# First-pass experts five to eight of the second mixture moved from hand-written units to the plan, with their weight sums split ahead

## The chip, the cores and the metric

One core of a Trainium2 chip runs the whole program in one launch. The metric is device time in microseconds (us): the median of three runs. A profiled execution of the same program gives the rows below; its own time and its span (first to last instruction) stand in the table.

## What is computed

Three layers, all in float32: a retention layer (4 batches, 8 heads, 576 positions of 64), a mixture with the best of eight experts for each token, and a mixture in which every token goes through all eight experts, weighted by a Sinkhorn-normalised gate. The third is most of the time:

```python
# x: 2304 x 512; w1: 8 x 512 x 1024; w2: 8 x 1024 x 512
out = np.zeros((N, D), dtype=np.float32)
for e in range(E):
    h = np.maximum(x @ w1[e], 0.0)
    ye = h @ w2[e]
    out += P[:, e:e + 1] * ye
```

## The kernel before

Every float32 operand is split into a high and a low part of a shorter format (ScalarE casts the high part, VectorE subtracts it from the operand for the low part: `lo_of`, L237), and a product is three matmuls, high x high, high x low and low x high.

**The second mixture** takes its 2304 tokens in three passes of 768, and in each pass the eight experts one after the other. The first product of an expert (`x @ w1`) is a 2 x 2 block product in seven instead of eight block products, from sums and differences of the blocks of `w1` ("sums") and of the tokens. The sums of one quarter of an expert's `w1` (i = 0 to 3) are 1792 columns, high and low. They are made once, in the first pass, and stored to DRAM in `w1s`; the later passes load them from there.

*First pass, hand-written units.* `unit` (L1243) is one quarter of one expert: seven block products (L1260 to L1262, 384 columns each, six matmuls to a product) and between them the second product of the quarter before (`second`, L1179; L1190 to L1192, 512 columns each, an ordinary product, nine matmuls for three token tiles at a time). There are 32 units. The order of a unit on TensorE is product 0, three token tiles of `second`, products 1 and 2, three tiles, product 3, three tiles, products 4 and 5, three tiles, product 6. Products 0, 2, 3 and 4 add up in one PSUM bank, which ScalarE copies out after 0, 2 and 3 (`keep`, L1238: `p1`, `u2`, `u3`); the next of these products waits for the copy. `mid` is called at named places ("p0", "b", ...) and runs what `mids` has for that place: the gate's steps and the tokens of the next pass.

*The ring.* Weights arrive by SP's DMA queue in five buffers of 512 KB (`raw`, `load_more`, L233) and are split into a ring of four slots (`split_step`; four steps to a slot). "plain" slots are cast as they are (L260); "sums" slots go through four sums on GpSimd (L271, L272) first (cast L279). A slot of first weights of the second mixture is stored to `w1s` at the start of its unit (L1248), high and low part, 896 KB each. `take` hands the next slot out and emits what is left of its splits; `release` gives a slot back. The first mixture uses the same ring for its own weights, four slots to an expert: two for `gemm1` (eight half-products of 12 matmuls with a ReLU after each), two for `gemm2`. A model of the two clocks (`clock`, `arrives`) decides where split steps are emitted.

*Second and third pass, planned.* From expert `s = E` on, every piece of work is a `Task` with an engine, a cost and predecessors. TensorE's order is written out (`line`); the other engines take the task with the earliest due time. A planned expert has the same first product (L1543 to L1545, weights `wa` loaded from `w1s` at L1510), and a second product that is also one of seven block products (L1690 to L1692, 256 columns each); its weights are combined on GpSimd (L1448, L1451) and split (L1636 on ScalarE, L237 on VectorE). `load_pass` brings in and splits the tokens of the next pass; between passes one and two that is done by the units (`xload`, `xsums`, and `xsplit` in the last unit through `renew`), between two and three by the plan. The buffers of the plan are laid over the ring and the work buffers of the units when these are done.

## Time and profile before

| | |
|---|---|
| median of 3 runs | 1811.48 us (1811.03 to 1811.97) |
| profiled execution, its own time | 1811.14 us |
| its span | 1809.4 us |
| TensorE matmul busy | 1785.6 us, 12398 matmuls |
| VectorE, ScalarE, GpSimd busy | 1244.2, 891.4, 409.4 us |
| DRAM read and written | 248.26 and 74.79 MB, 179 GB/s over the span |

The span has three parts: retention layer and first mixture up to 338 us, the first pass of the second mixture in units up to 842, the planned passes to the end. Matmuls are pipelined, so the busy time of TensorE says little; the starts of successive matmuls give what one costs. A line number alone belongs to the kernel before.

### The profile page before, as it was taken

The page shows a single profiled execution, that of the slowest core. Times are in us where ns is not written, and L with a number is a line of the kernel's source. Part 1 is how long each engine was busy: PE and PEld are TensorE (multiplying, and loading weights), DVE is VectorE, ACT ScalarE, POOL GpSimd, SP SyncE. Part 2 cuts the span into 40 slices and gives each one's busy share as a digit, 9 for nine tenths or more (in the row PEclk, how much of TensorE's full clock was granted, in tenths as well). Part 3 has the DMA queues.
Part 4 walks back from the last instruction along what each step waited for, and adds up shares of the span by engine and source line. Part 5 has one row for each costly group of instructions (what it writes and reads, how often), then busy time and mean ns, then how long its engine had stood idle before and what let it go on. Part 6 is the DMA issues. An engine that isn't in the chain of part 4 may idle for free.

```text
span 1809.4 us, 32670 instructions
## 1 busy us (share of the span) xinstructions
PE 1785.6 (99%) x12398; PEld 1705.3 (94%) x12398; DVE 1244.2 (69%) x2205; ACT 891.4 (49%) x1718; POOL 409.4 (23%) x396
## 2 busy tenths in 40 slices
PE   8999999999999999999999999999999999999998
PEld 7889999998999999998999999999999999999997
DVE  6764666557555655664667787787877777777777
ACT  2454455534443333343565555555656555555553
POOL 4630121221321212213221111111222112111212
PEclk9999999999999999999999999999999999999999
DMA  9854655564545556545755556555555555555540
GB/s 325 298 196 158 213 184 190 186 217 155 197 176 192 192 192 227 185 164 188 234 155 169 158 163 191 166 163 153 150 182 181 162 164 153 177 160 156 155 129 36
DMA packets 190597, 325.29 MB, mean 180 GB/s; under 512 B 20551, under 2 KB 93400, under 8 KB 190429
## 3 DMA queue, kind: packets, MB, share of 16 engines
q1 hardware_dynamic: 187132, 312.89, 53.2%
q0 software_dynamic: 3136, 9.95, 1.6%
q8 instruction: 100, 1.64, 0.4%
q14 instruction: 69, 0.56, 0.1%
q10 hardware_dynamic: 160, 0.26, 0.0%
HBM read 248.26 MB, written 74.79 MB: 179 GB/s over the span
## 4 chain that ended last, share of the span: by engine, by line
PE 86%; DVE 3%; issue 2%; ACT 1%; POOL 0%; POOLq 0%; DVEq 0%; ACTq 0%
PE b L1543 8%; PE b L1545 8%; PE b L1544 8%; PE b L1692 8%; PE b L1691 8%; PE b L1690 8%; PE b L1190 5%; PE b L1192 5%; PE b L1191 5%; PE b L1260 4%; PE b L1261 4%; PE b L1262 4%; PE b L722 4%; PE b L724 3%; PE b L723 3%
## 5 line engine op out<-in xcount | busy, mean ns | idle before, releaser
L1691 PE MATMUL b<-wb,sq 128*128 128x256 f32 x1344 | 378.5, 282 | 1.1 <-DVE wb L237 1.1
L1690 PE MATMUL b<-wb,sq 128*128 128x256 f32 x1344 | 377.1, 281 | 0.9 <-DVE a L1712 0.9
L1692 PE MATMUL b<-wb,sq 128*128 128x256 f32 x1344 | 377.1, 281 | 0.4 <-DVE sq L237 0.4
L1691 PEld LDWEIGHTS b<-wb,sq 128*128 128x128 f32 x1344 | 254.0, 189 | 1.7 <-DVE wb L237 1.7
L1692 PEld LDWEIGHTS b<-wb,sq 128*128 128x128 f32 x1344 | 254.4, 189 | 0.6 <-DVE sq L237 0.6
L1690 PEld LDWEIGHTS b<-wb,sq 128*128 128x128 f32 x1344 | 252.9, 188 | 1.8 <-issue 1.3
L237 DVE TENSOR_TENSOR ring<-raw,ring 128x512 fp32r<-128x512 f32 (+1 forms) x256 | 192.5, 761 | 69.2 <-ACT ring L260 61.0
L237 DVE TENSOR_TENSOR sq<-hq,sq 128x768 fp32r<-128x768 f32 x167 | 168.8, 1015 | 68.3 <-ACT sq L1636 68.2
L1448 POOL TENSOR_TENSOR raw<-raw,raw 128x512 f32<-128x512 f32 x60 | 84.8, 1414 | 384.2 <-DVE wb L237 313.3
L1558 ACT ACTIVATE hq<-hq 128x384 f32<-128x384 f32 x144 | 75.6, 526 | 184.4 <-DVE hq L1555 183.7
L1543 PE MATMUL b<-ch,wa 128*128 128x384 f32 x448 | 151.4, 338 | 2.2 <-DVE hq L1555 1.6
L1260 PE MATMUL b<-ch,ring 128*128 128x384 f32 x448 | 152.5, 340 | 0.2
L1543 PE MATMUL b<-c,wa 128*128 128x384 f32 x448 | 151.2, 337 | 1.1 <-ACT u L1549 1.1
L1636 ACT CAST sq<-hq 128x768 fp32r<-128x768 f32 x167 | 137.6, 829 | 29.2 <-PE b L1691 24.5
L1545 PE MATMUL b<-ch,wa 128*128 128x384 f32 x448 | 150.6, 336 | 0.0
L1545 PE MATMUL b<-c,wa 128*128 128x384 f32 x448 | 150.6, 336 | 0.0
L1261 PE MATMUL b<-cl,ring 128*128 128x384 f32 x448 | 150.6, 336 | 0.0
L1262 PE MATMUL b<-ch,ring 128*128 128x384 f32 x448 | 150.6, 336 | 0.0
L1544 PE MATMUL b<-cl,wa 128*128 128x384 f32 x448 | 150.6, 336 | 0.0
L1544 PE MATMUL b<-c,wa 128*128 128x384 f32 x448 | 150.5, 336 | 0.0
L1190 PE MATMUL b<-ring,HH 128*128 128x512 f32 x384 | 149.8, 390 | 0.0
L1192 PE MATMUL b<-ring,HL 128*128 128x512 f32 x384 | 149.5, 389 | 0.0
(258 smaller groups left out, 4179.5 us busy)
## 6 DMA issues: line engine op xcount, KB each, us to landing
wa<-w1s SPq DMA_DIRECT2D x192, 512.0 KB, 4.2
raw<-in_moe_w_dram SPq DMA_DIRECT2D x128, 512.0 KB, 3.9
w1s<-ring SPq DMA_DIRECT2D x64, 896.0 KB, 5.9
raw<-in_moe_w_dram SPq DMA_DIRECT2D x106, 256.0 KB, 3.5
wa<-w1s SPq DMA_DIRECT2D x64, 256.0 KB
sums<-in_moe_w_dram SPq DMA_DIRECT2D x22, 256.0 KB, 3.2
xs<-x SPq DMA_DIRECT2D x19, 256.0 KB, 4.8
kT<-in_kT_dram SPq DMA_DIRECT2D x18, 256.0 KB, 4.0
```

Source lines behind the costliest of these rows:

```text
L237: eng.tensor_tensor(lo, x, hi.bitcast(F32), ALU.subtract)
L1190: nc.tensor.matmul(y[t], hh[:, s], w.hi[:, f0:f0 + 512], start=first, stop=False)
L1192: nc.tensor.matmul(y[t], hl[:, s], w.hi[:, f0:f0 + 512], start=False, stop=end)
L1260: nc.tensor.matmul(ps, a, xh[:, r, :], start=first and r == 0, stop=False, skip_group_check=True)
L1261: nc.tensor.matmul(ps, a, xl[:, r, :], start=False, stop=False, skip_group_check=True)
L1262: nc.tensor.matmul(ps, b, xh[:, r, :], start=False, stop=r == 1, skip_group_check=True)
L1543: nc.tensor.matmul(ps, a, xh[:, r, :], start=first, stop=False, skip_group_check=True)
L1544: nc.tensor.matmul(ps, a, xl_[:, r, :], start=False, stop=False, skip_group_check=True)
L1545: nc.tensor.matmul(ps, b, xh[:, r, :], start=False, stop=r == 1, skip_group_check=True)
L1690: nc.tensor.matmul(ps, hh[:, r, c], wh[:, r], start=st, stop=False, skip_group_check=True)
L1691: nc.tensor.matmul(ps, hh[:, r, c], wl[:, r], start=False, stop=False, skip_group_check=True)
L1692: nc.tensor.matmul(ps, hl[:, r, c], wh[:, r], start=False, stop=kh == 1 and r == 1, skip_group_check=True)
```

## The change

- The plan begins at expert `S0 = 4` of the first pass (it was `E`, the first expert of the second pass). There are 16 units instead of 32. The tokens of the second pass are now brought in by `load_pass`, in the plan; `renew`, the token loads in `mids` and the flag `last` go.
- The sums of the first weights of experts 4 to 7 (16 quarters) have to be in `w1s` before the plan loads them. Eight of them are made in the first mixture, as extra slots of the ring (`make_ahead`; `MADE_IN` says how many in which expert): loaded, summed, split like a unit's slot and stored at once by `store_sums`, then the slot is free again. Ring slots are now handed out from a list of free ones.
- The other eight are made beside units 9 to 16 with buffers of their own (`side_tiles`: two load buffers `er`, one for sums `ez`, two for the split `ec`). In unit k of these, at "p0" to "p3", piece s is cast and subtracted (`side_cut`) and the piece before is stored (`side_store`); at "p4" the last piece is stored and the weights of two units later are loaded; at "d" GpSimd makes the next sums. The source is read in rows of 128 columns (512 bytes).

```diff
+    S0 = 4
+    MADE_IN = (0, 1, 2, 2, 1, 1, 1, 0)
...
+    made = [(e, i) for e in range(S0, E) for i in range(4)]
+
+    def make_ahead():
+        e, i = made.pop(0)
...
+        Slot("sums", [part((e, i, 0), source)], 0, store=4 * e + i)
 
     for i in range(E):
         w1_slots(i)
-        w2_slots(i)
...
+        for f in range(2):
+            if MADE_IN[i] > f:
+                make_ahead()
+            w2_slot(i, f)
+    for e in range(S0):
...
+    ring_free, held = [1, 0, 2, 3], []
...
-            if j >= min(len(slots), n_rel[0] + RING):
+            if j >= len(slots) or (s == 0 and not ring_free):
                 return
...
             if s == 0:
-                c.hi, c.lo = (ringt[j % RING][:, 2048 * n:2048 * (n + 1)] for n in range(2))
+                c.ring = ring_free.pop(0)
+                c.hi, c.lo = (ringt[c.ring][:, 2048 * n:2048 * (n + 1)] for n in range(2))
...
             n_split[0] += 1
+            if s == 3 and c.store is not None:
+                store_sums(c, c.store)
+                ring_free.append(c.ring)
...
+    def store_sums(c, n):
+        for k, x in enumerate((c.hi, c.lo)):
+            nc.sync.dma_start(out=w1s[n][:, k], in_=x[:, 0:1792].bitcast(F32))
+        arrives(5.2)
...
+    def side_load(k):
+        if 0 <= k < len(made):
+            e, i = made[k]
+            for h in range(2):
+                nc.sync.dma_start(out=aside["raw"][k % 2][:, h], in_=w21[e][:, h * half + 128 * i:h * half + 128 * (i + 1)]
+                                  .rearrange("(k p) f -> p k f", p=128))
+            arrives(1.46)
+
+    def side_sums(k):
+        if 0 <= k < len(made):
+            first_sums(aside["z"], *(aside["raw"][k % 2][:, h] for h in range(2)))
+
+    def side_cut(k, s):
+        fa, fb = (aside["raw"][k % 2][:, h] for h in range(2))
+        z = aside["z"]
+        x = (fa, fb[:, 2:4], z[:, 0:4], z[:, 4:8])[s]
+        n = 128 * x.shape[1]
+        hi, lo = (aside["cut"][s % 2][:, h, 0:n].rearrange("p (j f) -> p j f", f=128) for h in range(2))
+        nc.scalar.copy(hi, x)
+        lo_of(nc.vector, lo, x, hi)
+
+    def side_store(k, s):
+        e, i = made[k]
+        o, n = ((0, 512), (1024, 256), (512, 512), (1280, 512))[s]
+        nc.sync.dma_start(out=w1s[4 * e + i][:, :, o:o + n], in_=aside["cut"][s % 2][:, :, 0:n].bitcast(F32))
+        arrives(1.5)
+
+    def side_mids(k):
+
+        def cut_at(s):
+            if s:
+                side_store(k, s - 1)
+            side_cut(k, s)
+        m = {} if k < 0 else {f"p{s}": (lambda _, s=s: cut_at(s)) for s in range(4)}
+
+        def end(_):
+            if k >= 0:
+                side_store(k, 3)
+            side_load(k + 2)
+            if k < 0:
+                side_load(k + 1)
+        m["p4"] = end
+        m["d"] = lambda _: side_sums(k + 1)
+        return m
...
-    n_unit = E * 4
+    n_unit = S0 * 4
...
-        elif p + 1 < NP and e == E - 3 and i == 3:
-            mids = {k: (lambda b, n=n: xload(p + 1, n)) for n, k in enumerate("bc")}
-        elif p + 1 < NP and e == E - 2 and i > 1:
-            mids = {"b": lambda b, n=i - 2: xsums(n)}
+        elif g >= n_unit - len(made) - 1:
+            mids = side_mids(g - n_unit + len(made))
...
-    for s in range(E, n_exp):
+    for s in range(S0, n_exp):
```

Two places in the order of instructions, both of the third expert of the first pass. First ScalarE in the tenth unit, from its first copy on (`c` are the copies p1, u2 and u3 out of PSUM bank `b0`, `HH` a ReLU, `ring` the splits). Before:

```order
L1238 COPY c_7320<-b0_7313 128x384
L279 CAST ring3_71<-raw4_67 128x512
L1228 ACTIVATE HH_111<-c_7347 128x384
L279 CAST ring3_71<-raw0_63 128x256
L1238 COPY c_7359<-b0_7313 128x384
L279 CAST ring3_71<-sums_84 128x512
L1238 COPY c_7378<-b0_7313 128x384
```

With the change (`er`, `ez` and `ec` are the side stream's buffers):

```order
L1278 COPY c_7482<-b0_7475 128x384
L1400 CAST ec0_6344<-er1_6342 128x512
L308 CAST ring3_71<-raw2_65 128x512
L1268 ACTIVATE HH_111<-c_7511 128x384
L308 CAST ring3_71<-raw3_66 128x256
L1400 CAST ec1_6345<-er1_6342 128x256
L1278 COPY c_7526<-b0_7475 128x384
L1400 CAST ec0_6344<-ez_6343 128x512
L308 CAST ring3_71<-sums_84 128x512
L1278 COPY c_7548<-b0_7475 128x384
```

A cast of the side stream now stands behind each copy or ahead of it; the third one, which writes `ec0` again, stands between the copies u2 and u3.

Then SP's queue from the ninth unit's pair of stores on (`w1s<-ring x2` is a unit's pair; loads of `raw` stand between the pairs). Before, up to the pairs of the tenth and eleventh unit:

```order
L1248 DMA w1s_90<-ring0_78 128x1792 x2
L233 DMA raw0_63<-in_moe2_w1_dram 128x4x256
L233 DMA raw1_64<-in_moe2_w2_dram 128x2x512
L233 DMA raw2_65<-in_moe2_w2_dram 128x2x512
L233 DMA raw3_66<-in_moe2_w1_dram 128x4x256
L1248 DMA w1s_90<-ring1_79 128x1792 x2
L1248 DMA w1s_90<-ring3_71 128x1792 x2
```

With the change, up to the pair of the tenth unit:

```order
L318 DMA w1s_90<-ring1_79 128x1792 x2
L254 DMA raw3_66<-in_moe2_w1_dram 128x4x256
L254 DMA raw4_67<-in_moe2_w2_dram 128x2x512
L1406 DMA w1s_90<-ec0_6344 256x1x512
L1406 DMA w1s_90<-ec1_6345 256x1x256
L1406 DMA w1s_90<-ec0_6344 256x1x512
L254 DMA raw0_63<-in_moe2_w2_dram 128x2x512
L254 DMA raw1_64<-in_moe2_w1_dram 128x4x256
L1406 DMA w1s_90<-ec1_6345 256x1x512
L1386 DMA er0_6341<-in_moe2_w1_dram 128x4x128 x2
L318 DMA w1s_90<-ring2_80 128x1792 x2
```

Four stores and two loads of the side stream now stand between two pairs; two loads of `raw` stand ahead of the unit's first side store and two ahead of its fourth, and the next unit's pair stands behind the side loads.

## Rows read from the trace of the kernel before

**Rows 1.** The page, part 1, whole span: engines' busy time, share, instructions; TensorE's clock by slices

```profile
span 1809.4 us, 32670 instructions
...
PE 1785.6 (99%) x12398; PEld 1705.3 (94%) x12398; DVE 1244.2 (69%) x2205; ACT 891.4 (49%) x1718; POOL 409.4 (23%) x396
...
PEclk9999999999999999999999999999999999999999
```

**Rows 2.** Stretches: from:to, length, busy PE, PEld, DVE, ACT, POOL (instructions), clock, DMA, GB/s

```profile
470.08:841.66 371.58, 371.58 (x1874) 336.66 (x1874) 216.80 (x346) 149.90 (x312) 80.52 (x95) 1.00 0.51 183
882.28:1235.88 353.60, 353.60 (x2521) 353.60 (x2521) 263.91 (x401) 193.09 (x346) 60.26 (x47) 1.00 0.55 167
1235.88:1356.41 120.53, 119.05 (x842) 118.22 (x841) 99.58 (x149) 67.92 (x119) 30.26 (x24) 1.00 0.54 164
...
173.00:236.00 63.00, 63.00 (x435) 60.94 (x434) 36.11 (x59) 30.91 (x64) 9.97 (x8) 1.00 0.61 201
```

**Rows 3.** Time line of TensorE, second products of a unit and a planned expert: start, length

```profile
661.06 0.39 PE L1190 MATMUL b<-ring,HH 128*128 128x512 f32 x1
...
663.10 0.34 PE L1260 MATMUL b<-ch,ring 128*128 128x384 f32 x1
...
1200.78 0.28 PE L1690 MATMUL b<-wb,sq 128*128 128x256 f32 x1
...
1201.49 0.34 PE L1543 MATMUL b<-ch,wa 128*128 128x384 f32 x1
```

**Rows 4.** Waits of TensorE, 841 to 884: waiter, releaser, sum, count, longest

```profile
PE b L1543 <- DVE hq L1555: 1.6, 2, 1.0
PE b L1543 <- ACT u L1549: 0.6, 1, 0.6
```

**Rows 5.** Time line of TensorE and ScalarE, one unit

```profile
655.88 0.34 PE L1260 MATMUL b<-ch,ring 128*128 128x384 f32 x1
...
661.30 0.60 ACT L260 CAST ring<-raw 128x512 fp32r<-128x512 f32 x1
661.81 0.47 ACT L1238 COPY c<-b 128x384 f32<-128x384 f32 x1
...
666.18 0.34 PE L1260 MATMUL b<-ch,ring 128*128 128x384 f32 x1
```

**Rows 6.** Time line of SP, two issues

```profile
669.24 0.37 SPq L233 DMA_DIRECT2D raw<-in_moe_w_dram  x1
...
680.89 1.05 SPq L1248 DMA_DIRECT2D w1s<-ring  x2
```

**Rows 7.** DMA issues of 470 to 840: count, KB each, median us from issue to landing

```profile
w1s<-ring SPq DMA_DIRECT2D x46, 896.0 KB, 5.9
raw<-in_moe_w_dram SPq DMA_DIRECT2D x42, 512.0 KB, 3.8
```

**Rows 8.** Stretches in which only stores, 1 KB loads, 2 KB loads move (columns of rows 2)

```profile
681.70:686.00 4.30, 4.30 (x24) 3.85 (x23) 2.15 (x3) 1.27 (x3) 2.84 (x4) 1.00 1.02 427
686.50:688.00 1.50, 1.50 (x10) 1.50 (x10) 1.15 (x3) 0.31 (x2) 0.00 (x0) 1.00 0.90 300
720.20:721.20 1.00, 1.00 (x6) 0.85 (x5) 0.80 (x2) 0.44 (x1) 0.00 (x0) 1.00 1.00 383
```

**Rows 9.** Time line of GpSimd and VectorE, a sum and two subtractions

```profile
661.74 1.06 POOL L271 TENSOR_TENSOR sums<-raw,sums 128x256 f32<-128x256 f32 x1
...
662.12 1.22 DVE L237 TENSOR_TENSOR ring<-raw,ring 128x512 fp32r<-128x512 f32 x1
...
668.52 0.69 DVE L237 TENSOR_TENSOR ring<-raw,ring 128x512 fp32r<-128x512 f32 x1
```

110 lines of the change are left out of this document (61 added, 49 removed).

## The prediction

> **What bounds the kernel now.** I read the first part of the page first, to see that TensorE is busy for 99% of an 1809.4 us span at the full clock, with the others far below [rows 1]. So a change gains only by fewer or shorter matmuls and loses only where TensorE is made to wait. Then the table by stretches: each row has its length, and the matmuls in brackets behind PE's busy time. Six experts of the hand-written part take 371.58 us, 61.93 each, with 1874 matmuls (312 each and two at the edge); six planned experts take 353.60 us, 58.93 each, with 2521 (420 each) [rows 2]. The planned expert has more matmuls and is shorter. The time line of TensorE says why: nine matmuls of 512 columns start within 2.04 us, 0.227 each, and six of 256 columns within 0.71 us, 0.118 each [rows 3]. A second product takes 144 of the first kind (32.7 us) in a unit expert, 252 of the second (29.8 us) in a planned one. The first product is the same in both.
>
> **The sum, part by part.** It is made against the profiled execution (1811.14 us, span 1809.4, so 1.74 around it); the median of the runs, 1811.48, lies 0.34 above it.
>
> *Four experts move to the plan.* 4 x (61.93 - 58.93) = **-12.0 us** [rows 2]. The hand-over itself, last unit beside first planned expert, occurs once in both kernels. By the Trainium skill ("TensorE: Matmul & The Clock Gate", Back-to-back issue gap) matmuls follow each other after N/2.4 + 2.5 ns, which is 216 and 109 ns, 3.6 us an expert and -14.2 for four (an estimate by that page). The rows have 227 and 118 with the weight loads, so they decide.
>
> *The change of token pass moves into the plan.* Between passes one and two the units split the new tokens in the last unit, and the stretch shows no loss. The planned change of pass costs 120.53 - 2 x 58.93 = 2.67 us [rows 2]; now there are two of these: **+2.7 us**.
>
> *Hand-over.* Now 0.62 and 1.6 us of waits stand there, on ScalarE and VectorE [rows 4]. The last unit loses seven token splits and gets four small cuts; the first planned loads of `wa` no longer wait for the ring slot that the last unit reads, but stand behind the side stream's last store on SP. A little earlier work on VectorE's queue: **-0.6**, between -2.2 (all of these waits) and +2.2 (as much again).
>
> *Eight sums in the first mixture's ring.* Each adds four casts, four subtractions, four GpSimd sums, a load of 512 KB and two stores of 896 KB. Experts three and four (63 us) get four of them. ScalarE is busy for 31 and VectorE for 36 of the 63 us, and stay under the span with four times 3 us more. The queue is the risk: its share is 0.61 [rows 2], 38.4 us, and each sum adds 4.3 us of stores and some 2 of load (rates below): 38.4 + 4 x 6.3 = 63.6 of 63 us. A ring slot just stored is split again four half-products later (12 matmuls of 0.145 each, 63 us over 435, so 7 us), against 5.9 us for a store to land [rows 7]; where a cast waits there, what stands behind it is ScalarE's last ReLUs before the second product, and TensorE goes on from other banks. With no load late the price is 0. With 7.6 us a sum instead of 6.3 the queue overflows by 5.8 us. Taken: **+1.0**, near the lower end, because slots are split a few us ahead of use.
>
> *The side stream.* In units 9 to 16, ScalarE casts a piece into one of two cut buffers, VectorE subtracts, SP stores, and the third cast needs the first store landed. That is the new wait, and behind it on ScalarE stand a split and then the copy `u3`, for which product 4 waits. In the trace the copy follows a split's cast by 0.51 us and takes 0.47, and product 4 starts at 666.18, 10.3 after the unit's start at 655.88 [rows 5]. So the third cast must start by 10.3 - 0.51 - 0.51 - 0.47 - 0.1 = 8.7 us into the unit. When does the store land? All loads and stores pass one queue in order. Its rates [rows 8]: 427 GB/s for the 896 KB stores (7 KB pieces), 383 for 2 KB pieces, 300 for 1 KB; so 4.3 us for a pair of stores, 1.4 for 512 KB in 2 KB pieces, 1.7 in 1 KB. The stores issued at 680.89 move from 681.7: 0.8 us to the first byte [rows 6, 8]. Side loads come in 512-byte pieces, which this trace lacks: at least 1.2 us (the 427 GB/s row), at most 3.5 (twice the packets of a 1 KB load); I take 2.0, near the 1 KB row and below its rate. A landing counts 0.3 us after the last byte (0.2 to 1.3, the latter what 3.8 us for a 512 KB load to land [rows 7] leave over 0.8 and 1.7).
>
> Tenth unit: on SP a load of `raw` stands ahead of the ninth unit's fourth side store; such a load goes at 669.24, 13.4 into its unit [rows 6], and holds SP till then. It moves until 15.9; fourth piece 17.3; side loads 19.3; the next unit's pair 23.6; the first piece 25.0, landed 25.3, which is 9.8 into the tenth unit: **1.1 us late**. Eleventh: the fourth piece is released 3.7 us before the unit ends (cut behind `u3`), moves to -1.5, side loads 0.5, pair 4.8, two raw loads 7.9, first piece 9.3, landed 9.6: **0.9 late**. Units 12 and 13 repeat both; in unit 9 no side stores are ahead, and from unit 14 no raw loads stand there. 2 x 1.1 + 2 x 0.9 = **+4.0**; with every lower bound 0.4, with every upper one (3.6, 3.4, 0.3 a unit) 14.6.
>
> GpSimd's four sums (3.2 us) now run once more in each of the eight units; a subtraction beside them took 1.22 us where it takes 0.69 [rows 9]. Mostly VectorE has room; before product 6 there are 2 us for one add. A tenth of a us a unit: **+0.8** (0 to 4.2, one slowed subtraction in each).
>
> Sum: -12.0 + 2.7 - 0.6 + 1.0 + 4.0 + 0.8 = -4.1: 1807.0 against the profiled execution, **1807.4 us** against the median.
>
> **Rivals.** (a) *Everything hides*: with 0.4 for the loop and nothing for ring and GpSimd, -9.5, 1802.0 us. For it: the queue's share in the units is 0.51 [rows 2]. Against it: a side unit adds 0.5 MB of loads and 1.8 of stores to 183 GB/s x 15.5 us = 2.8 MB, 5.2 MB or 335 GB/s, between the 300 and the 383 of the rows. (b) *Late landings*: each store signals 1.8 us after its last byte instead of 0.3. Then the four units lose 2.6 and 2.4 us, 10.0 together, and the sum is +1.9, 1813.4 us, no change. For it: 5.9 us for a store to land, where 2.2 are its bytes [rows 7]; against: a part of that is the other store of the pair. The Trainium skill ("DMA: Bandwidth & Descriptors", Anatomy of one DMA) says this, that a completion waits for the write's receipt, most of some 2 us, longest for HBM. No row here separates it. (c) *Slower*: the loop from third cast to first store sets the pace, because 512-byte pieces are as slow as 1 KB ones and landings 1.3 us late: 14.6 us, sum +6.5, 1818.0 us. It decides from 11.7 us in all, 2.9 in each of the four units. (d) *The four experts don't run at the planned pace*, because their weights come late while the side stream's stores drain: nothing gained, about 1811.5. Against it: all sixteen sums are stored by the end of the last unit, and a stretch of planned experts has a queue share of 0.55 [rows 2].
>
> **Chances.** Forecast 0.40 (own range 1804 to 1810.5), (a) 0.25, (b) 0.17, (c) 0.13, (d) 0.05. A measurement tells about 0.2% (3.6 us) from no change: faster is below 1807.9. That holds all of (a) and some 0.6 of the forecast: 0.50. Slower is (c): 0.13. The rest is 0.37. The range: 1801.6 (the lower bounds) to 1814.5 (over (b)) leaves out (c) and little more.
>
> **What would show it.** Matmuls of 512 columns halve, 432 matmuls more; the planned experts five to eight at 58.9 us; a second 2.7 us at the change of pass in expert nine; in units 10 to 13 a wait of TensorE on the copy behind the third cast, itself waiting for the store of the first piece, 15.5 becoming 16.4 to 16.6; the first mixture at most 1 to 2 us longer. I am wrong if the side units keep 15.5 us (a), or stretch by over 2 us (b, c), or if TensorE waits for split weights in the first mixture.

## The result, and the profile after

The changed kernel takes 1825.07 us (median of 4 runs, 1824.38 to 1826.19) beside 1811.72 for the kernel before: a ratio of 1.0074, 95% interval 1.0057 to 1.0091. It is slower by 13.4 us, 0.7%. The profiled execution took 1824.71 us; its span is 13.5 us longer than that of [rows 1]. The page's first lines, the kernel after:

```profile
span 1822.9 us, 34087 instructions
...
PE 1783.8 (98%) x12830; PEld 1722.0 (94%) x12830; DVE 1322.3 (73%) x2320; ACT 947.9 (52%) x1798; POOL 453.0 (25%) x421
...
PEclk9999999999999999999999999999999999999999
```

There are 432 matmuls more, as forecast, in 1.8 us less of busy time, and the span is longer all the same: TensorE waits, and for some us its granted clock is lower. The table by stretches tells where it went (columns as in [rows 2]): first mixture, units 1 to 8, units 9 to 12, units 13 to 16, and two planned experts of the first pass:

```profile
121.65:348.75 227.10, 217.43 (x1511) 208.40 (x1510) 144.98 (x242) 127.78 (x266) 65.24 (x62) 0.99 0.77 266
348.75:481.30 132.55, 132.33 (x716) 120.13 (x715) 84.51 (x176) 58.18 (x123) 36.70 (x43) 1.00 0.60 210
481.30:553.82 72.52, 67.15 (x314) 59.68 (x314) 46.49 (x76) 32.33 (x68) 28.48 (x34) 0.93 0.79 278
553.82:616.44 62.62, 62.47 (x313) 55.88 (x313) 41.95 (x68) 29.89 (x62) 18.41 (x21) 1.00 0.75 275
656.87:774.79 117.92, 117.92 (x842) 117.92 (x842) 89.25 (x137) 61.73 (x110) 18.29 (x15) 1.00 0.57 179
```

and the first mixture of the kernel before:

```profile
119.65:337.70 218.05, 215.14 (x1512) 207.12 (x1510) 127.90 (x210) 114.00 (x234) 37.35 (x30) 1.00 0.59 192
```

The sum of the 13.5 us, from the starts of the first matmul of each stretch in the two traces: the first mixture starts 2.0 us later (121.65 against 119.65) and is 9.05 longer; units 1 to 8 are 0.2 longer, units 9 to 16 take 135.14 instead of 2 x 61.93 = 123.86, 11.3 longer; the hand-over is 0.2 shorter (40.42 against 40.62); four planned experts for four experts of units give -12.0; the added change of pass costs 2.40 (61.33 - 58.93); four small places in the planned part add 0.8. That is 2.0 + 9.05 + 0.2 + 11.3 - 0.2 - 12.0 + 2.4 + 0.8 = 13.55.

**First mixture.** TensorE's waits there (121 to 348 us; waiter, releaser, sum, count, longest):

```profile
PE b L762 <- DVE h L784: 8.0, 7, 2.6
PE b L762 <- PEq L888: 1.7, 1, 1.7
```

The same waits of TensorE in the kernel before:

```profile
PE b L722 <- PEq L848: 1.5, 1, 1.5
PE b L722 <- DVE h L744: 1.2, 3, 0.5
```

And those of ScalarE and VectorE with the change:

```profile
ACT ring L289 <- DMA raw<-in_moe_w_dram: 10.7, 6, 2.8
ACT ring L308 <- POOL sums L261: 8.9, 3, 5.4
...
ACT ring L308 <- DMA w1s<-ring: 2.2, 1, 2.2
ACT ring L289 <- DMA w1s<-ring: 1.6, 1, 1.6
```

```profile
DVE ring L258 <- DMA w1s<-ring: 7.0, 2, 3.5
```

TensorE waits 8.0 us for the low part of a ReLU's result (`h`, L784 on VectorE); before, the same wait was 1.2. The other line is a branch on a flag, at which TensorE waits in every kernel here. ScalarE waits for loads, for GpSimd's sums and for stores out of a ring slot. How one comes from the other shows at the largest loss, where TensorE waits twice:

```profile
252.93 0.41 PE L762 MATMUL b<-HH,ring 128*128 128x304 f32 x1 [2.58 <-DVE h L784]
...
257.08 0.41 PE L762 MATMUL b<-HH,ring 128*128 128x304 f32 x1 [2.23 <-DVE h L784]
```

The time lines of VectorE, ScalarE and GpSimd there:

```profile
246.54 1.29 DVE L258 TENSOR_TENSOR ring<-raw,ring 128x512 fp32r<-128x512 f32 x2
...
248.62 3.87 DVE L258 TENSOR_TENSOR ring<-raw,ring 128x512 fp32r<-128x512 f32 x2 [0.40 <-ACT ring L308]
252.41 0.46 DVE L784 SCALAR_TENSOR_TENSOR h<-b,h 128x304 fp32r<-128x304 f32 x1
```

```profile
248.80 0.42 ACT L783 ACTIVATE h<-b 128x304 fp32r<-128x304 f32 x1
254.62 1.31 ACT L308 CAST ring<-sums 128x512 fp32r<-128x512 f32 x2 [5.39 <-POOL sums L261]
255.83 0.42 ACT L783 ACTIVATE h<-b 128x304 fp32r<-128x304 f32 x1
```

```profile
248.16 1.84 POOL L258 TENSOR_TENSOR cl<-x,ch 128x768 fp32r<-128x768 f32 x1 [7.62 <-ACT ch L1115]
250.08 2.13 POOL L1096 TENSOR_TENSOR x<-x 128x768 f32<-128x768 f32 x1
252.17 0.90 POOL L262 TENSOR_TENSOR sums<-raw 128x256 f32<-128x256 f32 x1
```

GpSimd first works on the next layer's tokens (248.16 to 252.2), then on the sums. The first wait comes by VectorE: the ReLU's high part is done at 249.2, but ahead of its low part (252.41) stand two subtractions of the made slot, which take 3.87 us beside GpSimd's work on the tokens, where two of the same line took 1.29 shortly before. The second wait comes by ScalarE: it stands 5.39 us in front of the cast of the sums, and the ReLU behind it (255.83) is the one for which TensorE waits until 257.08. All six profiles with this order of sums have both waits (2.4 to 2.7 us and 0.7 to 2.2). Behind the second one the matmuls run at the lower clock for some us, half of which are lost:

```profile
258.20:261.50 3.30, 3.30 (x15) 3.30 (x15) 2.18 (x5) 1.66 (x3) 0.00 (x0) 0.50 0.76 313
```

So a split whose result the plan loads over 350 us later (its first loads of `wa` go out at 611.8) holds up a ReLU that is needed now, on two engines.

**Units 9 to 16.** TensorE's waits from 481 to 617 us, and then the tenth unit (it starts at 496.86) on SP, ScalarE and TensorE:

```profile
PE b L1298 <- ACT c L1278: 5.3, 2, 3.3
```

```profile
495.46 0.53 SPq L1406 DMA_DIRECT2D w1s<-ec  x1
496.08 1.87 SPq L1386 DMA_DIRECT2D er<-in_moe_w_dram  x2
498.00 1.23 SPq L318 DMA_DIRECT2D w1s<-ring  x2
501.38 9.78 SPq L1406 DMA_DIRECT2D w1s<-ec  x4
```

```profile
503.49 0.47 ACT L1278 COPY c<-b 128x384 f32<-128x384 f32 x1
507.85 0.62 ACT L1400 CAST ec<-ez 128x512 fp32r<-128x512 f32 x1 [3.89 <-DMA w1s<-ec]
508.38 0.61 ACT L308 CAST ring<-sums 128x512 fp32r<-128x512 f32 x1
508.90 0.47 ACT L1278 COPY c<-b 128x384 f32<-128x384 f32 x1
```

```profile
509.42 0.44 PE L1298 MATMUL b<-ch,ring 128*128 128x384 f32 x1 [2.02 <-ACT c L1278]
...
510.75 0.50 PE L1299 MATMUL b<-cl,ring 128*128 128x384 f32 x1
511.06 0.52 PE L1300 MATMUL b<-ch,ring 128*128 128x384 f32 x1
```

This is the mechanism that the prediction described: the first piece goes to SP's queue at 501.38, behind the pair of stores (498.00), it lands at 507.85, 10.99 into the unit, and copy `u3` and product 4 come behind the third cast. What the prediction did not have is the last fence: 1.3 us after the wait the matmuls come every 0.32 us instead of the usual 0.174 for 384 columns. The granted clock in two stretches behind the two waits:

```profile
510.60:514.00 3.40, 3.40 (x11) 3.05 (x10) 2.72 (x6) 1.81 (x4) 2.63 (x4) 0.52 0.99 327
546.40:551.80 5.40, 5.40 (x17) 5.01 (x16) 3.55 (x6) 2.24 (x5) 4.01 (x5) 0.51 0.97 325
```

0.52 and 0.51 of full speed is the lower level, 1.2 GHz. Of the 11.5 us by which matmul starts in units 9 to 16 are further apart than their usual pitch, 4.2 are matmuls at the lower clock, 6.3 the four gaps of over 0.15 us, and the rest small ones. The two large gaps are 2.2 and 3.5 us beyond the pitch (the views count from the modelled end of the matmul before: 2.02 and 3.3). So a wait of 2.2 us cost about 4, and one of 3.5 about 6.

### The profile page after: what moved, and what is told of

It is laid out like the page before. It is cut to its first block, busy times and chain, and to the rows that moved or that the text cites. A ratio compares the mean times of both kernels' runs of the same rounds, so it can differ in the third digit from the quotient of the medians.

```text
span 1822.9 us, 34087 instructions
## 1 busy us (share of the span) xinstructions
PE 1783.8 (98%) x12830; PEld 1722.0 (94%) x12830; DVE 1322.3 (73%) x2320; ACT 947.9 (52%) x1798; POOL 453.0 (25%) x421
## 4 chain that ended last, share of the span: by engine, by line
PE 76%; DVE 7%; DMA 3%; issue 3%; ACT 2%; POOL 1%; POOLq 0%; SPq 0%; ACTq 0%; DVEq 0%
PE b L1623 10%; PE b L1625 10%; PE b L1624 10%; PE b L1772 10%; PE b L1771 10%; PE b L1770 10%; PE b L762 2%; PE b L764 2%; PE b L763 2%; DMA raw<-in_moe_w_dram 2%; PE b L1298 2%; PE b L1230 2%; PE b L1231 2%; PE b L1232 2%; PE b L1300 2%
## 5 line engine op out<-in xcount | busy, mean ns | idle before, releaser
L1771 PE MATMUL b<-wb,sq 128*128 128x256 f32 x1680 | 473.0, 282 | 1.1 <-DVE wb L258 1.1
L1772 PE MATMUL b<-wb,sq 128*128 128x256 f32 x1680 | 471.5, 281 | 0.8 <-DVE sq L258 0.8
L1770 PE MATMUL b<-wb,sq 128*128 128x256 f32 x1680 | 471.2, 280 | 0.9 <-DVE a L1792 0.9
L1772 PEld LDWEIGHTS b<-wb,sq 128*128 128x128 f32 x1680 | 318.0, 189 | 1.2 <-DVE sq L258 1.2
L1771 PEld LDWEIGHTS b<-wb,sq 128*128 128x128 f32 x1680 | 317.5, 189 | 1.7 <-DVE wb L258 1.7
L1770 PEld LDWEIGHTS b<-wb,sq 128*128 128x128 f32 x1680 | 316.1, 188 | 1.8 <-issue 1.3
L1623 PE MATMUL b<-c,wa 128*128 128x384 f32 x896 | 302.7, 338 | 2.3 <-ACT u L1629 2.1
L1625 PE MATMUL b<-c,wa 128*128 128x384 f32 x896 | 301.2, 336 | 0.0
L1624 PE MATMUL b<-c,wa 128*128 128x384 f32 x896 | 301.1, 336 | 0.0
L258 DVE TENSOR_TENSOR ring<-raw,ring 128x512 fp32r<-128x512 f32 (+1 forms) x208 | 150.9, 745 | 51.3 <-ACT ring L289 31.1
L1792 DVE SCALAR_TENSOR_TENSOR a<-b,P,a 128x256 f32<-128x256 f32 x306 | 141.3, 478 | 49.6 <-PE b L1772 48.8
L258 DVE TENSOR_TENSOR wb<-raw,wb 128x512 fp32r<-128x512 f32 x231 | 162.8, 706 | 18.6 <-ACT wb L1716 18.6
L1623 PEld LDWEIGHTS b<-c,wa 128*128 128x128 f32 x896 | 169.1, 189 | 3.7 <-ACT u L1629 2.9
L1625 PEld LDWEIGHTS b<-c,wa 128*128 128x128 f32 x896 | 168.4, 188 | 0.0
L1624 PEld LDWEIGHTS b<-c,wa 128*128 128x128 f32 x896 | 168.3, 188 | 0.0
L1716 ACT CAST wb<-raw 128x512 fp32r<-128x512 f32 x231 | 142.6, 618 | 45.9 <-PE b L1772 44.6
L1629 ACT COPY u<-b 128x384 f32<-128x384 f32 x160 | 76.4, 477 | 73.2 <-PE b L1625 72.4
L289 ACT CAST ring<-raw 128x512 fp32r<-128x512 f32 x160 | 95.1, 620 | 15.7 <-DMA raw<-in_moe_w_dram 12.9
```

Of the source, the lines that this page charges most:

```text
L258: eng.tensor_tensor(lo, x, hi.bitcast(F32), ALU.subtract)
L289: nc.scalar.copy(c.hi[:, o:o + 512], x[:, i:i + 512])
L1623: nc.tensor.matmul(ps, a, xh[:, r, :], start=first, stop=False, skip_group_check=True)
L1624: nc.tensor.matmul(ps, a, xl_[:, r, :], start=False, stop=False, skip_group_check=True)
L1625: nc.tensor.matmul(ps, b, xh[:, r, :], start=False, stop=r == 1, skip_group_check=True)
L1716: nc.scalar.copy(o.tile[0], src.tile)
```

## The experiments

One table for all, from the starts of the first matmuls as above (us): start and length of the first mixture, units 9 to 16 (123.86 without loss; with S0 = 6 units 17 to 24), the hand-over expert, the median, and the ratio to the kernel before, measured beside it, with its interval.

| kernel | start | first mixture | units | hand-over | median | ratio |
|---|---|---|---|---|---|---|
| before | 119.65 | 218.05 | 123.86 | 40.62 | 1811.72 | 1 |
| the change | 121.65 | 227.10 | 135.14 | 40.42 | 1825.07 | 1.0074 (1.0057 to 1.0091) |
| made_stored_later | 120.17 | 226.42 | 137.50 | 40.73 | 1824.26 | 1.0062 (1.0045 to 1.0079) |
| made_no_sum | 120.30 | 222.88 | 137.19 | 40.71 | 1821.35 | 1.0055 (1.0034 to 1.0075) |
| made_load_only | 118.95 | 221.36 | 136.80 | 40.36 | 1818.00 | 1.0033 (1.0021 to 1.0044) |
| made_dve_sums | 122.87 | 224.78 | 138.06 | 40.45 | 1824.68 | 1.0061 (1.0046 to 1.0077) |
| four_ones | 120.94 | 223.19 | 137.63 | 40.37 | 1823.76 | 1.0062 (1.0046 to 1.0079) |
| six_side | 119.09 | 218.32 | 138.12 | 43.36 | 1825.49 | 1.0075 (1.0058 to 1.0092) |
| pair_after | 123.15 | 226.85 | 130.31 | 42.22 | 1823.53 | 1.0063 (1.0047 to 1.0080) |
| late_cut | 119.35 | 229.65 | 147.33 | 40.82 | 1835.48 | 1.0125 (1.0104 to 1.0146) |
| ones_late_pair | 122.10 | 223.40 | 135.98 | 41.95 | 1826.46 | 1.0083 (1.0065 to 1.0101) |
| three_bufs | 119.46 | 226.29 | 127.84 | 40.32 | 1815.11 | 1.0020 (1.0010 to 1.0031) |
| three_pair | 121.90 | 228.68 | 135.66 | 42.06 | 1826.45 | 1.0074 (1.0058 to 1.0091) |
| three_load | 122.88 | 227.52 | 129.22 | 40.55 | 1818.98 | 1.0026 (1.0015 to 1.0037) |
| three_pair_m | 120.91 | 221.21 | 133.04 | 40.67 | 1818.93 | 1.0045 (1.0028 to 1.0062) |
| six_three_pair | 120.22 | 218.10 | 131.10 | 45.07 | 1819.08 | 1.0042 (1.0028 to 1.0056) |
| three_m | 119.23 | 222.10 | 127.62 | 40.56 | 1811.29 | 0.9997 (0.9986 to 1.0008) |
| three_load_m | 121.85 | 224.39 | 128.78 | 40.31 | 1813.24 | 1.0001 (0.9992 to 1.0010) |
| three_load_m7 | 121.40 | 220.95 | 129.35 | 40.31 | 1811.91 | 0.9997 (0.9987 to 1.0006) |
| three_m7 | 121.51 | 224.06 | 127.59 | 40.32 | 1811.20 | 0.9996 (0.9987 to 1.0006) |

Two things on reading it. The start of the first mixture lies anywhere from 118.95 to 123.15, also among kernels whose instructions up to there are the same (the change, 121.65; late_cut, 119.35), so the 2.0 us of the change are not put down to it. And six profiles with the change's own first mixture (the change, pair_after, late_cut, three_bufs, three_pair, three_load) give 226.3 to 229.65: one profile tells that stage to some 2 us. So it is with the units: the six profiles with the change's own side stream (the change, the four made_ runs and four_ones) give 135.14 to 138.06, a loss of 11.3 to 14.2 us, of which the change's is the smallest. The profiled execution of three_pair took 1832.18 us, 5.7 above its median.

### What the sums made in the first mixture cost

**made_stored_later**: not stored there, but by units 1 to 8 out of their own slots.

```diff
+    unstored = []
...
             if s == 3 and c.store is not None:
-                store_sums(c, c.store)
+                unstored.append(c.store)
+                arrives(5.2)
                 ring_free.append(c.ring)
...
         store_sums(w, 4 * u["e"] + u["i"])
+        if unstored:
+            store_sums(w, unstored.pop(0))
```

> The eight sums made in the first mixture are loaded, summed and split there as before, but not stored there; units 1 to 8 each store their own sums once more in their place, so those eight parts of w1s hold wrong sums. Theory 1 (the splits that reuse a ring slot wait for its store to land, and hold ReLUs behind them): the waits on w1s<-ring (10.8 us on ScalarE and VectorE) go, and of the 9.4 us that the first mixture is longer than before 5 or more go: about 1819 us. Theory 2 (GpSimd's sums come late and ScalarE stands behind them): the waits on sums (8.9 us on ScalarE) stay and at least 6 of the 9.4 us stay. Theory 3 (bytes: weights of the first mixture land late because the queue carries more): as theory 1 in time, but then the waits on raw (10.7 us against 4.1 before) fall with it. Units 1 to 8 have room in the queue; more than 2 us lost there is not expected.

The waits on stores went from the first mixture, with them most of those on loads (2.5 us are left of 10.7), and TensorE's waits for ReLUs fell from 8.0 to 5.2 us. But 226.42 us is inside what the change's own order gives. A part of that is chance: behind the branch at 141 us the matmuls ran at the lower clock here (0.65 from 141.3 to 146.1), which cost 1.5 us or more and which the change's profile does not have at that place. So the 5 us of theory 1 fall, and theory 3 with them as far as the stores' bytes go; that the stores cost nothing isn't shown, up to some 3 us may be theirs. The wait on sums is still there (ScalarE's waits of this run):

```profile
ACT ring L309 <- POOL sums L262: 5.4, 1, 5.4
```

**made_no_sum**: casts and subtractions take the loaded columns instead of the sums.

```diff
-                if s == 0:
+                if s == 0 and c.store is not None:
+                    c.sums = raws[c.parts[0]][2].rearrange("p (j f) -> p j f", f=128)
+                elif s == 0:
                     c.sums = sumt.rearrange("p (j f) -> p j f", f=128)
```

> The sums of the eight quarters made in the first mixture are left out: the loaded columns are split and stored instead of them, so eight parts of w1s hold wrong values; all loads, splits and stores stay. Theory 1 (stores landing late): the first mixture keeps at least 6 of its 9.4 us. Theory 2 (ScalarE waits for GpSimd's sums ahead of a ReLU): the 8.9 us of waits on sums go and 4 or more of the 9.4 us with them: about 1820 us. Theory 3 (bytes): nothing changes, 1825.

222.88, 4.2 us of the 9 are gone (3.4 to 6.8 against the spread of that order). So theory 2 has what it asked for, 4 us or more, which is about half of the loss, and the 6 us of theory 1 don't stay. What is left has other names among ScalarE's waits:

```profile
ACT ring L289 <- DMA raw<-in_moe_w_dram: 12.4, 4, 4.2
ACT ring L310 <- DMA w1s<-ring: 3.3, 1, 3.3
```

**made_load_only**: on top of made_stored_later, a made slot is skipped when its load is there.

```diff
+            if c.store is not None:
+                unstored.append(c.store)
+                arrives(5.2)
+                n_split[0] += 4
+                load_more()
+                continue
...
```

> The eight sums of the first mixture are loaded and not used there: no casts, subtractions, GpSimd sums or stores of them; units 1 to 8 store their own sums once more in their place, so eight parts of w1s are wrong. What is left is the load of 512 KB in 512-byte pieces and its place among the five load buffers. Theory A (the work and waits of the splits in ScalarE's and VectorE's order): the first mixture is within 1.5 us of before (219.5 or less), 1817 us. Theory C (the load buffers and the queue: weights of the first mixture arrive later because a made load stands ahead of them): at least half of the 9 us stay (222.5 or more), 1820 us or more.

221.36 lies between the two bounds, 3.3 us over before. But most of these 3.3 are not where a made slot is split. TensorE's waits of this run:

```profile
PE b L770 <- PEq L896: 2.7, 1, 2.7
PE b L770 <- DVE h L792: 1.8, 3, 0.9
```

The branch (L896 here) takes 2.7 us in this profile, 1.4 to 2.1 in all others, also in those with nothing made in this stage, and behind it the matmuls run at the lower clock (0.50 from 141.6 to 144.8). Measured by the starts of matmuls against before, 2.8 us are lost there and 0.6 at 251. Whether the loads lengthen the branch one profile doesn't tell; what they cost elsewhere is below 1 us, as theory A had it, and 5.7 us or more hang on the splits, sums and stores. Of the 1818 us the rest is the side stream's 12.9.

**four_ones**: `MADE_IN = (1, 1, 1, 1, 1, 1, 1, 1)`.

> The eight sums of the first mixture are made one in each expert (MADE_IN all 1) instead of two in the third and fourth. All of the loss there lay in three stretches (near 211, 243 to 260 and 310 us), most of it at 243 to 260, where the kernel before has three short waits already. Theory A (a tight place: the splits of two made slots in a row stand ahead of ReLUs where ScalarE, VectorE and GpSimd also split the first layer's tokens for the next): with one made slot an expert the first mixture is 3 to 6 us longer than before instead of 9; 1820 us. Theory B (each made sum costs about 1.1 us wherever it is): 9 us again, 1825. Units as in the change.

223.19, 5.1 over before, as theory A had it: the waits at 250 us are those of the kernel before, and what is lost stands elsewhere (1.3 us at 123, 1.9 behind the branch at 143, at the lower clock, and a wait of 2.0 at 344, where a split stands ahead of the first unit's product). The last sum also falls on the first unit, which grows from 19.56 to 21.79, so the whole gains little.

**made_dve_sums**: the made slots' sums on VectorE.

```diff
-    def first_sums(z, fa, fb):
-        sub = lambda o, a, b: nc.gpsimd.tensor_tensor(o, a, b, ALU.subtract)
-        nc.gpsimd.tensor_tensor(z[:, 4:6], fb[:, 0:2], fb[:, 2:4], ALU.add)
+    def first_sums(z, fa, fb, eng=nc.gpsimd):
+        sub = lambda o, a, b: eng.tensor_tensor(o, a, b, ALU.subtract)
+        eng.tensor_tensor(z[:, 4:6], fb[:, 0:2], fb[:, 2:4], ALU.add)
...
-                    first_sums(c.sums, fa, fb)
+                    first_sums(c.sums, fa, fb, nc.gpsimd if c.store is None else nc.vector)
```

> The change with one edit: the four sums of each quarter made in the first mixture run on VectorE instead of GpSimd (units and side stream as before on GpSimd). If the loss comes from GpSimd's order (sums behind the token work, ScalarE's casts and ReLUs behind the sums), ScalarE's 8.9 us of waits on these sums shrink to under 2 and the first mixture is 4 to 6 us longer than before instead of 9: 1820 to 1821 us. If the work itself is too much for the stretch, VectorE's added 2 us a sum make it as long as in the change or longer: 1825 or more.

The wait on sums halves and doesn't go, because they now stand in VectorE's order:

```profile
ACT ring L308 <- DVE sums L261: 4.3, 3, 3.0
```

The first mixture, 224.78, is 6.7 longer than before: 1.5 to 4.9 us better than the change's order, and the whole time is the change's (1.0061). That GpSimd's order is one cause stands; that it is the only one doesn't. GpSimd's work on the tokens, beside which the subtractions were slow, stayed where it was in all these runs: its part is read from the time lines and not tested by itself.

**six_side**: eight sums only, all in the side stream.

```diff
-    S0 = 4
-    MADE_IN = (0, 1, 2, 2, 1, 1, 1, 0)
+    S0 = 6
+    MADE_IN = (0, 0, 0, 0, 0, 0, 0, 0)
...
-            if e == E - 3 and i == 0:
+            if e == max(E - 3, S0) and i == 0:
                 xlast = [P_[0]]
```

> The plan begins at expert seven of the first pass (S0 = 6) and nothing is made in the first mixture: eight sums beside units 17 to 24, with the side stream as in the change. If the first mixture's loss comes from the sums made there, the first unit begins at 337.7 to 338.5 as before; the 1.8 us that the retention layer was longer tell whether they belong to the first loads of these sums (they go) or not (they stay). The side stream loses its 10 to 11 us again: 1811.7 - 6.0 (two experts) + 2.4 (change of pass) - 0.2 + 11 = 1819 us. If the loss in the side stream's units came from what the made sums had left in the queue, it shrinks to 4 or less and the time is 1812 or below.

First mixture 218.32, as before to 0.3 us: the 9 us come from the made sums, all of them. But units 17 to 24, with the same side stream and an undisturbed queue ahead of it, lose 14.3 us, and the hand-over 2.7, of which the cause wasn't looked for: the side stream's price is its own.

### What the side stream costs

**pair_after**: the unit's pair of stores goes out behind the second piece.

```diff
         w = take()
-        store_sums(w, 4 * u["e"] + u["i"])
...
         u2 = keep(xb, "u2")
         mid("p2", None)
+        store_sums(w, 4 * u["e"] + u["i"])
```

> The unit's own pair of stores goes to SP's queue behind the second piece of the side stream instead of at the unit's start. Theory 1 (the third cast waits for the first piece's store, which stands behind the pair's 4.3 us in the one queue): the first piece lands some 4 us after its cut, the third cast no longer waits, units 9 to 16 take 15.5 us each, the four experts of units 62 us instead of 72.5 and 62.6 for the last two, and the whole 1825.1 - 10.5 = 1814.5 us. Theory 2 (the queue simply has too many bytes in these units, or GpSimd's and VectorE's extra work is the brake): the wait moves to another piece or to the ring, experts three and four keep at least half of their 11 us, 1819 us or more. The first mixture stays as it was.

The units lose 6.4 instead of 11.3 and the hand-over 1.8 more (the last pair now stands ahead of the planned loads of `wa`). The sixteenth unit, at whose end TensorE waits for `wa`, takes 18.1 us instead of 15.5; without it 3.8 us are left, so neither theory alone. TensorE's waits from 483 to 616 us:

```profile
PE b L1623 <- DMA wa<-w1s: 2.4, 1, 2.4
PE b L1297 <- ACT c L1278: 1.5, 3, 0.9
```

The third cast of the tenth unit still waits 2.24 us for the first piece: two loads of raw, the fourth piece and the side loads stand ahead of it in the queue.

**late_cut**: third and fourth cast one place later, with their stores and the side loads.

```diff
...
-        m = {} if k < 0 else {f"p{s}": (lambda _, s=s: cut_at(s)) for s in range(4)}
+        m = {} if k < 0 else {p: (lambda _, s=s, c=c: at(s, c)) for p, s, c in (
+            ("p0", None, 0), ("p1", 0, 1), ("p2", 1, None), ("p3", None, 2), ("p4", 2, 3))}
...
```

> The third and fourth piece of the side stream are cut one place later (behind the copy u3, and at the place behind product 4), their stores and the side loads one place later too. Nothing is taken off the queue. Theory 1 (what costs is only that the third cast, waiting for a store, stands ahead of the copy for which product 4 waits): a landing 11 or 12 us into the unit does no harm any more, units 9 to 16 take 15.5 to 15.7 us, experts three and four 62.0 to 62.6 each, about 1815 us. Theory 2 (the queue is full of the unit's bytes, and the wait only moves): the landings get later with the later stores, TensorE waits for the ReLU behind product 4 or for the ring, and 5 us or more of the 11.3 stay: 1819 us or more.

10 us slower than the change. The copy `u3` is free, but the wait has moved to VectorE: its subtraction stands behind the cast, and behind the subtraction the add of product 5 (L1266), for which product 6 waits. TensorE's waits from 481 to 628 us:

```profile
PE b L1298 <- DVE c L1266: 12.5, 5, 4.6
PE b L1298 <- ACT c L1278: 0.7, 1, 0.7
```

That is theory 2's form of it (the wait moves), at a larger price.

**ones_late_pair** joined late_cut, pair_after and four_ones.

> Three edits together: one made sum in each expert, the third and fourth piece cut one place later, the unit's pair of stores behind the second piece's. By theory 1 for the units (order in the queue and on ScalarE) they lose under 1 us, and by theory A the first mixture loses 3 to 6: 1811.7 - 12 + 2.4 - 0.2 + 0.3 + 4.5 + 0.5 = 1807 us, which would beat both kernels. By theory 2 and B 5 and 9 us stay: 1816.

It had the parts' faults: 12.1 us in the units, 1.3 at the hand-over and 3.1 in units 1 to 8. In the units TensorE waits 3.4 us for the planned load of `wa`, 2.5 once for a copy, behind a first cast that waits 4.1 us for the fourth piece's landing, and five times 0.7 to 0.8 us for copies and VectorE's adds.

**three_bufs**: the low parts of the first two pieces are written over their source, so the same 8 KB of cut buffers (per partition) hold three buffers, and the third cast needn't wait for a store of its unit.

```diff
-        aside["cut"] = [q.tile([128, 2, 512], F32R, name=f"ec{i}") for i in range(2)]
+        aside["cut"] = [q.tile([128, n, 512], F32R, name=f"ec{i}") for i, n in enumerate((1, 1, 2))]
...
-        hi, lo = (aside["cut"][s % 2][:, h, 0:n].rearrange("p (j f) -> p j f", f=128) for h in range(2))
+        ca, cb, cc = aside["cut"]
+        hi, lo = ((ca[:, 0], None), (cb[:, 0, 0:256], None), (cc[:, 0], cc[:, 1]), (ca[:, 0], cb[:, 0]))[s]
+        hi = hi.rearrange("p (j f) -> p j f", f=128)
+        lo = x.bitcast(F32R) if lo is None else lo.rearrange("p (j f) -> p j f", f=128)
...
```

> Cut buffers laid out anew in the same memory: the low parts of the first two pieces are written over their source, so the third piece has a buffer of its own and waits for no store of its unit; the fourth takes the buffers of the first two and is the one that waits. All work, bytes and the order in the queue stay (seven issues a unit instead of four). Theory 1 (the loop third cast, first store): the fourth cast stands behind the copy u3, and may start up to 12.6 us into the unit (ahead of product 6 by a cast, a subtraction and an add: 14.45 - 0.5 - 0.7 - 0.6); landings at 11 to 12.5 us just meet that: units 9 to 16 lose 0 to 4 us in all instead of 11.3, 1815 to 1818 us. Theory 2 (the queue's backlog, with the wait moving on to VectorE as it did when the cuts were moved): 6 us or more stay, 1820 us or more.

The units lose 4.0, 1815.11 us in all: theory 1, at the upper end of its range, with the same work, bytes and order in the queue (seven issues a unit instead of four). The two later runs with these buffers and this order, three_m and three_m7, lose 3.8 and 3.7. Stretches of units 9 to 12 and 13 to 16, and TensorE's wait over both:

```profile
478.17:543.13 64.96, 62.70 (x313) 55.93 (x313) 45.30 (x76) 32.49 (x68) 25.41 (x30) 1.00 0.84 297
543.13:606.00 62.87, 62.16 (x313) 56.17 (x313) 42.26 (x70) 29.61 (x62) 21.45 (x25) 1.00 0.79 291
```

```profile
PE b L1298 <- ACT c L1278: 3.0, 4, 1.4
```

The queue moves more per us than in the change (297 against 278 GB/s) and TensorE waits less. The clock stays at 1.00: none of its waits is over 1.4 us by this view.

**three_pair**: three_bufs and pair_after.

> The buffers of the run before, and the unit's pair of stores behind the second piece's. Now the first two pieces stand behind at most two loads of raw, the fourth piece of the unit before and the side loads, and landed 10.2 us into the unit or earlier where only the pair was moved; the fourth cast has until 12.6. By theory 1 the units lose under 1 us, and what is left is the hand-over, where the last stores stand ahead of the planned loads (1.6 us lost there when only the pair was moved): 1825.1 - 11.3 + 1.0 + 1.6 = 1816 us, the first mixture's 9 us staying. If 4 us or more stay in the units, the bound is something other than this loop: the work on ScalarE, VectorE or GpSimd, or late weights.

Missed: 11.8 us in the units (9.2 in three_pair_m, which has the same side stream). In this arrangement the first cast of a unit takes the fourth piece's buffer of the unit before, and that piece now stands behind the pair. ScalarE in the tenth unit:

```profile
506.60 0.62 ACT L1403 CAST ec<-er 128x512 fp32r<-128x512 f32 x1 [2.75 <-DMA w1s<-ec]
```

The loop was closed again, over the end of the unit. And as in pair_after some 2 us of the loss are the wait for `wa` in the last unit. The moved pair costs in units 1 to 8 as well, where there is no side stream: 0.4 to 4.1 us in pair_after, three_pair, three_pair_m and six_three_pair.

**three_load**: three_bufs with the side loads behind the first piece of the next unit.

```diff
             side_cut(k, s)
+            if s == 1:
+                side_load(k + 1)
...
-            side_load(k + 2)
             if k < 0:
                 side_load(k + 1)
```

> three_bufs with the side loads moved from the end of a unit to behind the first piece's store in the next (the place p1): in the queue they no longer stand ahead of the unit's pair and the first two pieces. If the 4 us that are left in the units are the wait for pieces that these 2 us of loads hold up, they fall to under 1.5: 1812.5 us. If they come from the backlog of raw loads and pairs, 3 or more stay: 1815. A risk is that the sums of the next unit then wait for their load: it would show as GpSimd's wait for er and as a late third cast.

5.4 us in the units instead of 4.0 (4.9 and 5.5 in its two variants below): the side loads were not what is left. It shows mostly as the same wait for copies (3.3 us).

**six_three_pair**: six_side with three_pair's buffers and order.

> The plan from expert seven (S0 = 6), nothing made in the first mixture, with the buffers and the store order of the two runs before: eight sums beside units 17 to 24. By theory 1 the side stream's 14.3 us and the 2.7 at the hand-over fall to under 1 and 1.6: 1811.7 - 6.0 + 2.4 + 2.2 = 1810 us. By theory 2: 1816 or more.

7.3 in the units, 4.4 at the hand-over: between the two theories, with the order of three_pair; 2.5 of the 7.3 are the wait for `wa` in the last unit.

### Both together

**three_pair_m** (three_pair with `MADE_IN = (0, 2, 1, 1, 1, 2, 1, 0)`):

> As the run before, and the first mixture's sums in other experts: MADE_IN (0, 2, 1, 1, 1, 2, 1, 0). With one in each expert the middle experts lost nothing beyond what the kernel before has; the losses were at the very start, at 141 us, and at the end (342 to 345). If two in a row cost only where the first layer's last tokens and the gate fill the engines (243 to 260 us), the first mixture is now 1 to 3 us longer than before: 1811.7 - 12 + 2.4 - 0.2 + 2 + 2.6 = 1806.5 us, faster than both. If each pair of made sums costs 3 us or more wherever it is, 1812 us or more.

**three_m** (three_bufs with the same order of sums):

> The buffers of three_bufs with the unit's pair of stores at its old place, and MADE_IN (0, 2, 1, 1, 1, 2, 1, 0). If the first mixture's loss hangs on where the doubles stand, it is 3 us longer than before instead of 9 (as in the run that had this order of sums and the later pair), and the units lose 4: 1815.1 - 6 = 1809 us. If the loss there hung on the other order of the stores, 8 or 9 us stay and it is 1815.

**three_load_m** (three_load with it):

> Both: the side loads behind the first piece, and MADE_IN (0, 2, 1, 1, 1, 2, 1, 0). With 3 us lost in the first mixture and 1 in the units: 1811.7 - 12 + 2.4 - 0.2 + 0.6 + 3 + 1 = 1806.5 us, faster than both. With 9 and 4, no better than 1815.

**three_load_m7** (three_load with `MADE_IN = (0, 2, 1, 2, 1, 1, 1, 0)`):

> As three_load, with MADE_IN (0, 2, 1, 2, 1, 1, 1, 0): one double stands again in the fourth expert, ahead of 243 to 260 us. If it is this place that costs, the first mixture is 7 to 9 us longer than before (5 of them at 243 to 260) and the time is 4 to 6 us above the run with the doubles in the second and sixth expert. If a double costs the same everywhere, the two are equal within 2 us.

**three_m7** (three_bufs with that):

> three_bufs (side loads at their old place) with MADE_IN (0, 2, 1, 2, 1, 1, 1, 0). The parts measured apart: 4 us lost in the units, 2.9 in the first mixture: 1811.7 - 12 + 2.4 - 0.2 + 0.8 (the two ends of passes) + 2.9 + 3.9 = 1809.5 us, within 0.2% of the kernel before. If it were faster by over 0.2% it would beat both kernels; if the first mixture's loss does not carry over, 1812 or more.

Of these expectations the low figures were missed by 12 us (three_pair_m), 7 (three_load_m) and 2 (three_m); three_load_m7 is within 2 us of three_load_m, and three_m7 within 2 of its 1809.5. The first mixture is 3.2, 4.1 and 6.3 us longer than before with doubles in the second and sixth expert, 2.9 and 6.0 with doubles in the second and fourth. So in length the fourth expert is no worse than the sixth. Where the loss sits differs, by the starts of matmuls against before: behind the fourth expert's double at 244 to 256 us (2.5 and 5 us or more), behind the sixth's at 301 to 322 (2.9 to 6), behind the second's in no run, and in the change behind the third's (1.2 at 213) and the fourth's (6 at 246 to 262). So two neighbouring doubles each cost, and the second expert's double costs nothing; why there is not shown. With the same order twice (three_load_m7, three_m7) the length differs by 3.1 us, so more than "2.9 to 6.3 instead of 8 to 11.6" isn't told by these runs. three_m and three_m7 take 1811.29 and 1811.20 us, ratios of 0.9997 and 0.9996 with intervals across 1: 14 us better than the change, no different from the kernel before. No version beat it.

## Why the prediction was wrong

By its own steps:

- *Four experts move to the plan*, -12.0: shown. An expert in the plan takes 58.93 us, one in units 61.93; two of the moved ones take 117.92, 58.96 each.
- *The change of pass*, +2.7: 2.40.
- *Hand-over*, -0.6: -0.2.
- *Eight sums in the first mixture's ring*, +1.0: **this step failed.** It measured +9.05 in the change and 8 to 11.6 over six profiles of that order. The step asked whether the engines and the queue have room in sum (they have: ScalarE and VectorE 127.78 and 144.98 us busy of 227.10) and took "0 with no load late" for the lower end, near which it chose, because slots are split a few us ahead of use. It looked for the wait on a stored slot, and that was there (10.8 us of waits on ScalarE and VectorE), but it is the smaller part (made_stored_later). What it did not look at is what a made slot's own splits wait for, and what stands behind them: on ScalarE the cast waits for sums that stand behind GpSimd's work on the tokens, on VectorE the subtractions take three times as long beside that work, and behind both stand the two parts of a ReLU of the first mixture for which TensorE has no other work. The prediction priced a subtraction beside GpSimd for the side stream [rows 9], but not here. The sentence that "TensorE goes on from other banks" is what the rows refute: it waited 8.0 us for these results. Nor was it a wait for split weights, the sign that was named. Some 1.6 us of the 9.05 are the lower clock behind the waits.
- *The side stream*, +4.0 (0.4 to 14.6): the mechanism was right and **the size was off**, 11.3. The condition held almost to the tenth: third casts at 8.92 and 8.94 us into a unit (the eleventh and the fourteenth) cost 0.28 and 0.33, against the 8.7 worked out. In the tenth unit the third cast started at 10.99 instead of 9.8. Two things were mis-sized. The landings: the side loads' last packet ended 20.2 after the ninth unit's start (19.3 forecast), the pair's 24.5 (23.6), the first piece's 25.8 (25.0), and the cast that waited for it began 0.74 after that instead of 0.3; no row of the kernel before gave that 0.3. And the clock: waits of 2.2 and 3.5 us were each followed by some us at the lower level, 4.2 in sum, which was in no term. The loss also sat otherwise in this profile: 4.0 and 6.3 in the tenth and twelfth unit, 0.3 and 0 in the eleventh and thirteenth, perhaps because a unit that waits gives the queue time for the next. The five other profiles with the same side stream lost in all four, as forecast (2.0 to 4.1, 0.8 to 2.8, 4.9 to 5.5 and 1.9 to 2.4), and 12.9 to 14.2 in all.
- *GpSimd's sums beside the units*, +0.8: not seen by itself.

From the forecast's -4.1 to the measured +13.5 us of span are 17.6: 8.1 by the ring, 7.3 by the side stream, 2.0 by the start of the first mixture, which isn't put down to the change, and the rest small.

Among the rivals, (c) came nearest, slower by the loop from third cast to first store, with 14.6 us for it. The loop was right and its two reasons were not, so that the figure came near was luck. The 512-byte pieces were not slow: a stretch with little but them moves at 342 GB/s, above the 300 of the 1 KB pieces [rows 8]:

```profile
499.80:500.80 1.00, 1.00 (x7) 0.96 (x6) 1.00 (x2) 1.00 (x3) 0.45 (x1) 1.00 1.13 342
```

Nor did landings come 1.3 us late. For (b), 1.8 us from last byte to signal, the 0.74 of the tenth unit speaks against it. By the Trainium skill ("DMA: Bandwidth & Descriptors", Anatomy of one DMA, which tells of DMAs that GpSimd issues) the write's receipt is most of some 2 us; on SP's queue this trace does not agree, with the 0.74. The chances gave "slower" 0.13, because only the side stream was allowed to bring it about. The ring's own upper figure, an overflow of 5.8 us, would have made the sum +0.7, no change; the queue's bytes weren't what set its price, and no rival had the 9.05.

## What to carry to other kernels

Work done ahead is not free because the engines are idle in sum. In these traces a piece that waits (for a sum on a third engine, a load, a store's landing) holds back the urgent work that stands behind it on its engine, 5.39 us in one place, and a slow piece does the same; the price is read at that place and not from busy shares. When a wait is moved, look at every engine that the moved instruction's consumers stand on: late_cut freed a copy on ScalarE, and with the wait on VectorE the units lost twice as much. A buffer that a store drains should not be needed again within the queue's backlog; here one more buffer, out of memory that was there, gave back 7 of 11 us with the same bytes.

## What the runs showed of the hardware that was not expected

Two subtractions on VectorE took 3.87 us beside GpSimd's work on the tokens, where two took 1.29 shortly before; the same two took 3.9 in all six profiles with this order of sums.

After TensorE had waited 2.2 us (gap at 507.0) its matmuls went on at the full rate for 1.3 us and then at 0.52 of the clock for 3.4; after 3.5 us (542.1) they ran at half rate at once, for some 6. After the gaps of three_bufs, up to 1.6 us beyond the usual pitch, no matmul was slowed; but in six_side one of 2.7 us (655.3) wasn't followed by slow ones either, where one of 2.2 (619.6) was. In the first mixture waits of 1.8 (made_stored_later, 141 us) and 2.2 us (the change, 257) were followed by some 3 us at half the clock. So a wait of about 2 us may cost up to twice its length, and its length alone doesn't tell.

Loads in 512-byte pieces moved faster than those in 1 KB pieces, 342 against 300 GB/s in the stretches shown. Why is not known. Over the 2.1 us from its first packet to its last, with other pieces at both edges, one side load of 512 KB moves at 245 GB/s, close to the 2.0 us that the prediction took.

What stays open: how the 9 us of the first mixture divide between VectorE's slow subtractions, ScalarE's wait for sums, the loads and the stores; why the second expert's double costs nothing; why the branch at 141 us takes 1.4 to 2.7 us; and why the start of that stage varies by 4 us between kernels that are the same up to there.
